# Spectral filter plus GELU network on one core: tiles 4 to 15 transposed by DMA, and the loads, first activations and order of work rearranged

## The chip, the cores and the metric

The kernel runs on one core of a Trainium2 chip. The metric is the device time in microseconds (us) of one execution; the median over the runs shown stands for a kernel. A profile is a hardware trace of one such execution. Its span runs from the first to the last recorded instruction, and the execution's own time is a little longer than the span.

## The reference

The input `x` is 2048 rows of 640 values in bfloat16. Each row is normalised (`xn`), and three terms are added:

```python
def _layernorm(x, axis=-1, eps=1e-5):
    m = jnp.mean(x, axis=axis, keepdims=True)
    v = jnp.var(x, axis=axis, keepdims=True)
    return (x - m) / jnp.sqrt(v + eps)

def _A_ref(x, w_r, w_i):                       # spectral filter over the whole 2048 x 640 plane
    X = rfft2(x.astype(float32), axes=(-2, -1))
    X = X * (w_r + 1j * w_i)                   # w: 2048 x 321
    return irfft2(X, s=(2048, 640), axes=(-2, -1)).astype(bfloat16)

def _B_ref(x, w1, b1, w2, b2):                 # w1: 640 x 1536, w2: 1536 x 640
    h = gelu(einsum("bsd,df->bsf", x, w1) + b1)
    return einsum("bsf,fd->bsd", h, w2) + b2

xn = _layernorm(x)
return x + _A_ref(xn, w_r, w_i) + _B_ref(xn, w1, b1, w2, b2)
```

## The kernel before

**Tiles.** The 2048 rows are held as 16 tiles of 128 rows (tile `c` holds the rows `16 p + c`, one for each partition `p`). All matrix work is in bfloat16 with float32 sums in PSUM, which has eight banks.

**Normalisation.** For each tile VectorE makes two `bn_stats` (line 622) and one `bn_aggr` (line 624), GpSimd takes the power -1/2 (line 626), and VectorE writes the normalised tile into a buffer `xn` that holds a pair of tiles (line 650; there are two such buffers). Tile 0 comes in two halves with a DMA each (lines 553 to 555), so that its first `bn_stats` can start on the first half. Tile 1's sums are made by ScalarE instead: two activations with accumulation (lines 583 and 585) and a small GpSimd instruction (line 587).

**The transposed copy.** Layer 1 needs each tile with its 640 columns on the partitions, as `xnT`, five blocks of 128 by 128. For tiles 0 to 7 TensorE makes five transposes into PSUM (line 667), and VectorE or ScalarE copies the result to `xnT` (line 673). Tiles in `BYDMA`, 8 to 15, are transposed by one DMA each, issued by SyncE (line 655), from `xn` straight to `xnT`.

**Layer 1 and the activation.** Layer 1 goes in blocks of tiles (`BLOCKS`): four blocks of two tiles (0 and 1, 2 and 3, 4 and 5, 6 and 7) and two blocks of four. For each of 12 chunks of the 1536 columns, five matmuls of 128 x 128 weights against 256 (or 512) columns of `xnT` are summed in one PSUM bank; ScalarE applies GELU with the bias into `gT` (line 738). In block 0 the first three of the five partial sums are made for each tile by itself (lines 710 to 716), the last two for both (line 727).

**The transform.** The two-dimensional transform is a chain of small matrix products with constant tables. VectorE folds each pair of normalised tiles (lines 679 and 683). TensorE multiplies the folded pair by the table G (line 689, the "table sums", `a_ops`), and the result is copied to `XV`. When all 16 tiles are there, the steps b (table E, line 762), c (table M, line 780), the filter on VectorE (lines 805 and 809), and d (table N, line 814) follow; 16 DMA transposes on SyncE (line 830) bring the result back into `XV`. The last part multiplies by the table GE (line 847), unfolds on VectorE (lines 855 and 860) and multiplies by H (line 913).

**Layer 2 and the output.** Layer 2 sums 12 products for each tile (`W2`, line 895). The residual and b2 come through buffers `xo`: ScalarE writes b2 into them as float32 (line 883), and a GpSimd DMA adds `x` (line 901). For tiles in `KEEP` the layer-2 sum is made early and VectorE adds it into `xo` (line 907), so that only the product with H is left for the end; for the others, layer 2 and H are summed in the same PSUM bank. VectorE adds `xo` and writes the output tile (line 916), and SyncE stores it (line 919).

**Loads.** All loads are written once, in order. SyncE issues `x`, `W1` and the tables in one queue; the eight direct loads of the filter (16 rows of 10,272 bytes each, `load_direct`) are issued by GpSimd once the load of tile 4 has landed (line 574). `W2` comes in four quarters, all behind tile 1's second activation, which uses `W2`'s space (line 600). Ten mirrored filter loads, GE and H follow among the DMA transposes (`turned`, line 604).

**What sets the order.** The order on each engine is written out by a list scheduler when the kernel is built (`Sched.schedule`): it takes a cost for each operation and a landing time for each DMA (`LAND`, line 173), and picks among the ready operations by priority (`PRIO`, `FOLD`, `GP`). `gate` only orders an operation behind the planned start of another; `reads`, `writes` and `after` become semaphore waits. On the chip each engine works through its own list strictly in order.

Of the kernel before, what the change touches and what calls it, by code (L numbers as in the profile page):

```python
# [13 lines left out]
D = 640  # L14
# [75 lines left out]
def mm_us(n):  # L90
    return max(n / 2400.0 + 0.0027, 0.0265)
# [81 lines left out]
LAND = {"x0_0#0": 2.21, "x0_1#0": 2.21, "x1#0": 2.41, "w1_0#0": 3.22, "b1t#0": 2.89, "w1_1#0": 3.98, "x2#0": 4.36, "w1_2#0": 4.71, "w1_3#0": 5.24, "w1_4#0": 5.77, "g#0": 6.59, "x4#0": 6.92, "x6#0": 7.12, "x8#0": 7.31, "x10#0": 7.5, "x12#0": 7.69, "x14#0": 8.04, "b2#0": 8.65, "e#0": 9.53, "m#0": 10.11, "n#0": 10.62, "W0#0": 5.52, "W0#1": 6.15, "W0#2": 6.54, "W0#3": 6.83, "W1#0": 6.67, "W1#1": 7.22, "W1#2": 7.12, "W1#3": 7.67, "w2#0": 13.91, "w2#1": 15.43, "w2#2": 16.32, "w2#3": 17.2, "W0#4": 2.91, "W0#5": 2.91, "W0#6": 3.32, "W0#7": 2.75, "W0#8": 2.84, "W1#4": 3.26, "W1#5": 3.67, "W1#6": 4.09, "W1#7": 3.51, "W1#8": 3.86, "i#0": 3.77, "h#0": 4.59, "xnT8#0": 2.89, "xnT9#0": 2.89, "xnT10#0": 3.31, "xnT11#0": 3.05, "xnT12#0": 3.15, "xnT13#0": 2.89, "xnT14#0": 2.89, "xnT15#0": 2.89, "v0#0": 2.89, "v1#0": 2.89, "v2#0": 2.89, "v3#0": 2.89, "v4#0": 2.89, "v5#0": 2.89, "v6#0": 2.89, "v7#0": 2.89, "v8#0": 2.89, "v9#0": 2.89, "v10#0": 2.89, "v11#0": 2.89, "v12#0": 2.89, "v13#0": 2.89, "v14#0": 2.89, "v15#0": 2.89, "xo0#0": 4.54, "out#0": 2.3, "xo1#0": 7.6, "out#1": 2.3, "xo2#0": 4.88, "out#2": 2.3, "xo3#0": 5.22, "out#3": 2.3, "xo4#0": 5.56, "out#4": 2.3, "xo5#0": 7.94, "out#5": 2.3, "xo6#0": 8.28, "out#6": 2.3, "xo7#0": 5.9, "out#7": 2.3, "xo8#0": 6.24, "out#8": 2.3, "xo9#0": 6.58, "out#9": 2.3, "xo10#0": 4.54, "out#10": 2.3, "xo11#0": 4.88, "out#11": 2.3, "xo12#0": 4.54, "out#12": 2.3, "xo13#0": 6.92, "out#13": 2.3, "xo14#0": 7.26, "out#14": 2.3, "xo15#0": 4.88, "out#15": 2.14, "out#16": 2.3, "out#17": 2.3}  # L173
# [231 lines left out]
BYDMA = tuple(range(8, 16))  # L405
# [6 lines left out]
XASPLIT = ['01234', '01 23 4', '0123 4', '01 234', '01 234', '01 234', '01 234', '01234']  # L412
KEEP = (0, 2, 3, 4, 7, 8, 9, 13, 14)
HOME = tuple(sorted((KEEP + tuple(c for c in range(16) if c not in KEEP))[-8:], key=lambda c: (c not in KEEP, c)))
FOLD = (14.0, 2.2, -51.6, -6.5, -36.5, 14.2, 44.0, 25.3)
GP = (-104.5, 12.2, 81.5, -77.1, 20.9, 158.1)
WARM = 42


def bass_parallel_sum__spectral_gfnet__dense_activation_gelu__prompt_kernel(  # L420
# [21 lines left out]
    with ExitStack() as es:  # L442
# [25 lines left out]
        mom = sb("mom", [128, 2], F32)  # L468
# [94 lines left out]
        load_w1(4)  # L563
        load(gtab[:], const["G"], B_g, (8, 4096), issue=0.5)
        load_x(4, 2)
# [16 lines left out]
        B_s1, B_s2, B_v1 = Buf("s1"), Buf("s2"), Buf("v1")  # L582
        K.op([("act", 0.75)], 300, lambda e, _: e.activation(view(W2, 0, [[1, D]]), view(X, D, [[1, D]]), ACT.Copy, scale=-1.0 / D, accum_out=mom[:, 0:1]),
             reads=[B_x[1]], writes=[B_s1])
        square = K.op([("act", 0.75)], 300, lambda e, _: e.activation(view(W2, 0, [[1, D]]), view(X, D, [[1, D]]), ACT.Square, bias=mom[:, 0:1], accum_out=mom[:, 1:2]),
                      reads=[B_x[1], B_s1], writes=[B_s2])
        K.op([("pool", 0.12)], 500, lambda e, _: e.tensor_scalar(out=mv[:, 1, 1:2], in0=mom[:, 1:2], scalar1=1.0 / D, scalar2=1e-5, op0=ALU.mult, op1=ALU.add),
             reads=[B_s2], writes=[B_v1])
# [3 lines left out]
        load(b2bc[:], bass.AP(tensor=b2v.tensor, offset=b2v.offset, ap=[[0, 128], [1, D]]), B_b2b, (8, 1280))  # L592
        load(etab[:], const["E"], B_e, (8, 1600))
        load(mtab[:], const["M"], B_m, (8, 512))
        load(ntab[:], const["N"], B_n, (8, 384))
        for ri in range(2):
            for q in range(4):
                load_direct(ri, q)
        for h in range(4):
            load_w2(h, after=[square])  # L600
        turned = [[] for _ in range(4)]
# [14 lines left out]
        for c0, n in [(0, 1), (1, 1)] + [(c, 2) for c in range(2, 16, 2)]:  # L616
            pr = 100 - c0 / 2
            B_mv, B_r = Buf("mv") if c0 != 1 else B_v1, Buf("r")
            for c in range(c0, c0 + n) if c0 != 1 else ():
                B_st = Buf("st")  # L620
                for h in range(2):
                    K.op([("dve", 0.393)], pr, lambda e, _, c=c, h=h: e.bn_stats(stats[:, c, 6 * h:6 * h + 6], view(X, c * D + H2 * h, [[1, H2]])),  # L622
                         reads=[B_x[c]] if c else [B_x0[h]], writes=[B_st], gate=mv_ops[:1])
                mv_ops.append(K.op([("dve", 0.119)], pr, lambda e, _, c=c: e.bn_aggr(mv[:, c, :], stats[:, c, :]), reads=[B_st, B_eps], writes=[B_mv]))  # L624
            a, b = c0, c0 + n
            K.op([("pool", 0.65)], 500, lambda e, _, a=a, b=b: e.tensor_tensor(out=rstd[:, a:b], in0=mv[:, a:b, 1], in1=mhalf[:, a:b], op=ALU.pow),  # L626
                 reads=[B_mv, B_mh], writes=[B_r] + B_rs[a:b])

        for pair in range(8):
# [10 lines left out]
            for n in range(2):  # L640
# [4 lines left out]
                for j0, j1 in cuts:  # L645
                    b = Buf(f"xn_{c}_{j0}")
                    for j in range(j0, j1):
                        B_xn[j] = b
                    w = 128 * (j1 - j0)
                    o = K.op([("dve", 0.356 if w == D else 0.1 + w / 1900)], pr, lambda e, _, c=c, n=n, xnv=xnv, o0=128 * j0, w=w: e.tensor_scalar(  # L650
                        out=xnv(n, o0, [[1, w]]), in0=view(X, c * D + o0, [[1, w]]), scalar1=mv[:, c, 0:1] if c != 1 else mom[:, 0:1], scalar2=rstd[:, c:c + 1], op0=ALU.subtract if c != 1 else ALU.add, op1=ALU.mult),
                        reads=([B_x[c]] if c else B_x0) + [B_rs[c]], writes=[xn, b])
                norm_ops.append(o)
                if c in BYDMA:
# [3 lines left out]
                    if c % 2 and c > 8:  # L658
                        turned[(c - 9) // 2].append(TD[c])
# [50 lines left out]
        for j in range(3):  # L710
            for c in range(2):
                first[j, c] = pe([("128", NFC * mm_us(128))], 60 - c - j / 4, lambda j=j, c=c: [
                    (h0v(fc, c, 1), view(W1, F * j + 128 * fc, [[1, 128]]), xnT[:, c, j, :], j == c == 0 and fc % 2 == 0, False) for fc in range(NFC)],
                    reads=[B_w1s[j], B_xnj[c, j]], writes=h0, gate=([first[j - 1, c]] if j else []) + ([first[j, 0]] if c else []))
                l1_ops.append(first[j, c])
                l1_of.setdefault(0, []).append(l1_ops[-1])
        for bi, (c0, nt) in enumerate(BLOCKS):
            for fc in range(NFC):
# [6 lines left out]
                if not bi:  # L725
                    if fc % 2 == 0:
                        l1_ops.append(pe([("128", 4 * mm_us(256))], pr + 10, lambda fc=fc: [
                            (h0v(f, 0, 2), view(W1, F * j + 128 * f, [[1, 128]]), xnT[:, 0:2, j, :], False, j == 4) for f in (fc, fc + 1) for j in (3, 4)],
                            reads=[B_w1s[3], B_w1s[4]] + [B_xnj[c, j] for c in range(2) for j in (3, 4)], writes=[hps], gate=[first[2, 1]]))
                        l1_of[0].append(l1_ops[-1])  # L730
                else:
# [6 lines left out]
                K.op([("act", act_us(128 * nt, 1))], pr + PRIO["gelu"] + GP[bi], lambda e, _, c0=c0, nt=nt, fc=fc, hps=hps: e.activation(  # L738
                    gT[:, fc, 128 * c0:128 * (c0 + nt)], psb(hps.slot, [[1, 128 * nt]]) if c0 else h0v(fc, 0, 2), ACT.Gelu_apprx_tanh, bias=b1col[:, fc:fc + 1], scale=1.0),
                    reads=[hps, B_b1c], writes=[bg])  # L740

# [217 lines left out]
```

## Time and profile before

| | |
|---|---|
| median of 3 runs | 150.87 us (150.87 to 151.32) |
| profiled execution: time | 150.26 us |
| profiled execution: span | 148.5 us |
| TensorE busy (matmul) | 141.8 us, 95% of the span |
| VectorE, ScalarE, GpSimd busy | 111.7, 82.7, 26.8 us |
| granted TensorE clock | 1.00 throughout |

In the profile PE is the TensorE matmul, PEld its weight load, DVE is VectorE, ACT ScalarE, POOL GpSimd and SP SyncE; a "q" behind a name is that engine's queue of issues. A group of instructions is shown as line, engine, operation, output<-inputs, count, then busy time and the mean in ns of one. Most matmuls are issued through one helper, so they share line 501 and are told apart by the tiles they read: `xnT,W` is layer 1, `W,gT` layer 2, `gtab,T` the table sums, `ident,T` the transposes. Matmul durations overlap one another, so the time that one takes in a run of matmuls is its share of that run and not its own duration.

### The profile page before, as it was taken

The page shows a single profiled execution, that of the slowest core. Times are in us where ns is not written, and L with a number is a line of the kernel's source. Part 1 is how long each engine was busy: PE and PEld are TensorE (multiplying, and loading weights), DVE is VectorE, ACT ScalarE, POOL GpSimd, SP SyncE. Part 2 cuts the span into 40 slices and gives each one's busy share as a digit, 9 for nine tenths or more (in the row PEclk, how much of TensorE's full clock was granted, in tenths as well). Part 3 has the DMA queues.
Part 4 walks back from the last instruction along what each step waited for, and adds up shares of the span by engine and source line. Part 5 has one row for each costly group of instructions (what it writes and reads, how often), then busy time and mean ns, then how long its engine had stood idle before and what let it go on. Part 6 is the DMA issues. An engine that isn't in the chain of part 4 may idle for free.

```text
span 148.5 us, 4149 instructions
## 1 busy us (share of the span) xinstructions
PE 141.8 (95%) x1740; PEld 92.5 (62%) x1756; DVE 111.7 (75%) x234; ACT 82.7 (56%) x151; POOL 26.8 (18%) x46
## 2 busy tenths in 40 slices
PE   7799999999999999999999999999999999999992
PEld 7589999988565536446553454444566765665572
DVE  2479999999994259857965995974019999999731
ACT  3526999999999994852658737444612240111000
POOL 4313830121200199700040000000040000000000
DMA  4999999999868979999934166063536113322221
GB/s 101 311 404 404 337 229 227 279 195 137 145 132 158 247 158 257 266 268 206 110 83 98 29 123 31 18 120 76 104 67 156 49 44 115 111 88 81 95 93 46
DMA packets 28307, 23.00 MB, mean 155 GB/s; under 512 B 17792, under 2 KB 24320, under 8 KB 28160
## 3 DMA queue, kind: packets, MB, share of 16 engines
q1 hardware_dynamic: 25696, 16.17, 46.6%
q0 software_dynamic: 2592, 6.56, 19.4%
q8 instruction: 14, 0.23, 0.7%
q14 instruction: 5, 0.04, 0.1%
HBM read 13.54 MB, written 2.62 MB: 109 GB/s over the span
## 4 chain that ended last, share of the span: by engine, by line
PE 88%; DVE 4%; DMA 3%; issue 2%; SPq 1%; ACT 0%
PE ps L501 87%; DMA W<-in_B_w_dram 3%; PE ps L667 1%; DVE Wf L513 1%; DVE Wf L855 1%; SPq L496 1%; DVE W L916 1%; DVE X L907 1%; DVE Wf L860 0%; ACT xnT L512 0%
## 5 line engine op out<-in xcount | busy, mean ns | idle before, releaser
L501 PE MATMUL ps<-xnT,W 128*128 128x256 bf16 (+2 forms) x396 | 57.0, 295 | 0.9 <-DMA W<-in_B_w_dram 0.9
L501 PE MATMUL ps<-W,gT 128*128 128x512 bf16 (+3 forms) x382 | 55.3, 292 | 1.5 <-issue 1.1
L501 PEld LDWEIGHTS ps<-W,gT 128*128 128x128 bf16 x396 | 30.1, 98 | 23.3 <-issue 2.2
L501 PEld LDWEIGHTS ps<-xnT,W 128*128 128x128 bf16 x396 | 34.1, 98 | 16.0 <-issue 1.7
L738 ACT ACTIVATE gT<-ps,b1col 128x256 bf16<-128x256 f32 (+1 forms) x72 | 37.4, 593 | 6.4 <-PE ps L501 6.1
L512 ACT ACTIVATE Wf<-ps 128x960 bf16<-128x960 f32 (+1 forms) x7 | 6.2, 894 | 22.0 <-PE ps L501 22.0
L901 POOL DMA_DIRECT2D xnT<-in_A_x_dram x8 | 9.9, 2596 | 45.4 <-DMA XV<-U 32.6
L622 DVE BATCH_NORM_STATS2 stats<-X 128x6 f32<-128x320 bf16 x30 | 13.1, 472 | 2.5 <-DMA X<-in_A_x_dram 2.5
L512 ACT ACTIVATE Xb<-ps 128x960 bf16<-128x960 f32 (+1 forms) x8 | 9.2, 1189 | 8.3 <-PE ps L501 8.3
L805 DVE TENSOR_TENSOR T<-Y,Wf 128x1288 bf16<-128x1288 bf16 x16 | 12.5, 826 | 0.0
L513 DVE CAST Y<-ps 128x644 bf16<-128x644 f32 x8 | 6.6, 828 | 6.2 <-PE ps L501 6.2
L513 DVE CAST Wf<-ps 128x960 bf16<-128x960 f32 (+1 forms) x5 | 5.1, 1019 | 7.5 <-PE ps L501 7.5
L626 POOL TENSOR_TENSOR rstd<-mv,mhalf 128x2 f32<-128x2 f32 (+1 forms) x9 | 6.6, 732 | 22.3 <-DVE mv L624 22.2
L916 DVE TENSOR_TENSOR W<-ps,xnT 128x640 bf16<-128x640 f32 (+2 forms) x10 | 6.9, 689 | 4.1 <-PE ps L501 4.1
L901 POOL DMA_DIRECT2D X<-in_A_x_dram x8 | 7.2, 2106 | 11.9 <-ACT gT L738 11.9
L683 DVE TENSOR_TENSOR T<-T 128x512 bf16<-128x512 bf16 (+1 forms) x32 | 8.5, 318 | 0.1
L512 ACT ACTIVATE XV<-ps 128x512 bf16<-128x512 f32 (+3 forms) x9 | 7.7, 873 | 0.0
L501 PE MATMUL ps<-getab,XV 32*128 32x160 bf16 (+1 forms) x128 | 7.5, 242 | 0.0
L512 ACT ACTIVATE U<-ps 128x512 bf16<-128x512 f32 (+1 forms) x12 | 4.6, 434 | 4.9 <-PE ps L501 4.8
L512 ACT ACTIVATE Y<-ps 128x644 bf16<-128x644 f32 x8 | 5.7, 707 | 2.9 <-PE ps L501 2.9
L513 DVE CAST Xb<-ps 128x640 bf16<-128x640 f32 (+1 forms) x4 | 4.3, 1065 | 3.9 <-PE ps L501 3.9
L907 DVE TENSOR_TENSOR X<-ps,X 128x640 f32<-128x640 f32 x8 | 6.6, 822 | 0.8 <-PE ps L501 0.8
(58 smaller groups left out, 149.6 us busy)
## 6 DMA issues: line engine op xcount, KB each, us to landing
X<-in_A_x_dram POOLq DMA_DIRECT2D x8, 320.0 KB, 6.7
xnT<-in_A_x_dram POOLq DMA_DIRECT2D x8, 320.0 KB, 7.8
out_dram<-W SPq DMA_DIRECT2D x15, 160.0 KB, 1.8
X<-in_A_x_dram SPq DMA_DIRECT2D x7, 320.0 KB, 8.8
W<-in_B_w_dram SPq DMA_DIRECT2D x5, 384.0 KB, 5.7
W<-in_B_w_dram SPq DMA_DIRECT2D x4, 480.0 KB, 18.4
Wf<-in_A_w_r_dram POOLq DMA_DIRECT2D x4, 160.5 KB, 8.4
Wf<-in_A_w_i_dram POOLq DMA_DIRECT2D x4, 160.5 KB, 9.6
```

Of the source, the lines that this page charges most:

```text
L496: return K.op([(q, 0.7 if q == "pool" else issue)], prio, lambda e, _: e.dma_start(dst, src), writes=[buf], after=after, rows=rows, gate=g ...
L501: ins = e.matmul(o_, lhsT=lw, rhs=rh, start=st, stop=sp_, skip_group_check=True)
L512: return e.activation(dst(), src(), ACT.Copy, scale=scale)
L513: return e.tensor_copy(dst(), src())
L622: K.op([("dve", 0.393)], pr, lambda e, _, c=c, h=h: e.bn_stats(stats[:, c, 6 * h:6 * h + 6], view(X, c * D + H2 * h, [[1, H2]])), reads=[B ...
L626: K.op([("pool", 0.65)], 500, lambda e, _, a=a, b=b: e.tensor_tensor(out=rstd[:, a:b], in0=mv[:, a:b, 1], in1=mhalf[:, a:b], op=ALU.pow), ...
L683: ring_ops.append(K.op([("dve", dve_us(4 * w, 2))], pr, lambda e, _, op=op, x1v=x1v, xfv=xfv, o_=o_, o0=o0, o1=o1, w=w: e.tensor_tensor(ou ...
L738: K.op([("act", act_us(128 * nt, 1))], pr + PRIO["gelu"] + GP[bi], lambda e, _, c0=c0, nt=nt, fc=fc, hps=hps: e.activation(gT[:, fc, 128 * ...
L805: filt_ops.append(K.op([("dve", dve_us(4 * KP, 2))], pr, lambda e, _, k=k, Y=Y, TB=TB, pair=pair: e.tensor_tensor(out=view(TT, TB.slot * 8 ...
L901: xo_ops[c] = K.op([("pool", 0.9)], 51 - c / 20, lambda e, _, c=c, xov=xov: e.dma_start(xov(0, D), xv[:, c, :], accum_op=ALU.add), reads=[ ...
L907: kept_ops.append(K.op([("dve", dve_us(D))], 30, lambda e, _, kps=kps, xov=xov: e.tensor_tensor(out=xov(0, D), in0=psb(kps.slot, [[1, D]]) ...
L916: K.op([("dve", dve_us(w))], 95, lambda e, _, os_=os_, fps=fps, o0=o0, w=w, xov=xov, base=base: e.tensor_tensor(out=view(W1, OST + os_.slo ...
```

## The change

- `BYDMA` is tiles 4 to 15 instead of 8 to 15: twenty TensorE transposes and four copies go, four DMA transposes on SyncE come.
- Tile 0 is loaded by one DMA. Tile 1's sums are made by VectorE like those of all other tiles; the two activations and the small GpSimd instruction go. All normalising writes are ordered behind tile 1's `bn_aggr`.
- The load of tiles 4 and 5 is issued ahead of the table G.
- The eight direct filter loads move from GpSimd to SyncE, and they, b2, E, M, N and the first quarter of `W2` are ordered behind the transposes of tiles 5 and 7 (`soon[1]`); the other quarters are ordered behind those of tiles 9, 11 and 13, and the mirrored filter loads one pair of tiles later than before.
- In block 0 of layer 1 the first partial sum of tile 0 is cut in two, and the fourth partial sum of the first six chunks is made ahead of the rest. The first table sum on TensorE is ordered behind the start of the tenth activation (`GATE0`).
- `KEEP` has ten tiles instead of nine, and others than before. Four of the `xo` additions wait for all 16 back transposes instead of two (and two for the first four).
- The planner's landing times (from issue to landing) are other ones: the first fifth of the layer-1 weights, `w1_0`, goes from 3.22 to 4.45 us, a tile's DMA transpose (`xnT8`) from 2.89 to 3.03, the last quarter of `W2` from 17.2 to 3.58. Priorities, the order of the transform's steps (`CHAIN`) and the splitting of copies (`XASPLIT`) change too.

```diff
-BYDMA = tuple(range(8, 16))
+BYDMA = tuple(range(4, 16))
...
-PRIO = {"hps": 50.5, "gelu": 116.3, "pb": 85.6, "pc": 135.6, "filt": 315.5, "ipc": 126.3, "eps": 84.4, "fin": 46.0}
+PRIO = {"hps": -20.8, "gelu": 180.6, "pb": 117.8, "pc": 194.1, "filt": 253.3, "ipc": 67.0, "eps": 51.3, "fin": 20.7}
 AHEAD = 1
-CHAIN = 'b0 b1 c01 c00 b2 c10 d00 d01 c11 b3 b4 c20 d11 c21 d10 b5 d20 c31 c30 d21 d30 d31'.split()
...
-KEEP = (0, 2, 3, 4, 7, 8, 9, 13, 14)
+CHAIN = 'b0 b1 c01 c00 b2 c10 d01 d00 c11 b3 d11 d10 b4 c21 c20 b5 c30 d20 c31 d21 d30 d31'.split()
...
+KEEP = (1, 2, 3, 4, 5, 8, 9, 11, 12, 14)
...
+GATE0 = 9
...
-        B_x0 = [Buf(f"x0_{h}") for h in range(2)]
-        for h in range(2):
-            load(view(X, H2 * h, [[1, H2]]), xv[:, 0, H2 * h:H2 * h + H2], B_x0[h], (8, 640), issue=0.41)
+        load_x(0, 1)
         load_x(1, 1)
...
+        load_x(4, 2)
         load(gtab[:], const["G"], B_g, (8, 4096), issue=0.5)
-        load_x(4, 2)
...
-                           bass.AP(tensor=src.tensor, offset=src.offset + q * RUN, ap=[[128 * 321, 16], [1, RUN]]), B_w[ri], (1, 10272), q="pool", after=[x_ops[4]], prio=90))
+                           bass.AP(tensor=src.tensor, offset=src.offset + q * RUN, ap=[[128 * 321, 16], [1, RUN]]), B_w[ri], (1, 10272), gate=soon[1]))
...
-            load_w2(h, after=[square])
+            load_w2(h, gate=[soon[1], turned[0], turned[1], turned[2]][h])
...
-            load_mirror(*a, gate=turned[(0, 0, 1, 1, 1, 2, 2, 2, 3, 3)[k]])
+            load_mirror(*a, gate=turned[(1, 1, 2, 2, 2, 3, 3, 3, 3, 3)[k]])
...
-                    if c % 2 and c > 8:
-                        turned[(c - 9) // 2].append(TD[c])
+                    if c % 2:
+                        (turned[(c - 9) // 2] if c > 8 else soon[1]).append(TD[c])
...
+        for j, c, f0, f1 in ((0, 0, 0, 6), (0, 0, 6, 12), (0, 1, 0, 12), (1, 0, 0, 12), (1, 1, 0, 12), (2, 0, 0, 12), (2, 1, 0, 12)):
...
+                reads=[B_w1s[j], B_xnj[c, j]], writes=h0[f0 // 2:f1 // 2], gate=prev)
...
+                if not bi and fc == GATE0:
+                    a_ops[0].gate.append(g_op)
...
-            xo_ops[c].deps += v_ops[:4] if c in HOME[4:6] else v_ops if c in HOME[6:] else []
+            xo_ops[c].deps += v_ops if c in HOME[4:] else []
```

More of the change, by code (lines that the diff above doesn't have):

```diff
@@ L467, in bass_parallel_sum__spectral_gfnet__dense_activation_gelu__prompt_kernel @@
         mhalf = sb("mhalf", [128, 16], F32)
-        mom = sb("mom", [128, 2], F32)
         rstd = sb("rstd", [128, 16], F32)
@@ L580, in load_mirror @@
                            bass.AP(tensor=src.tensor, offset=src.offset + row * 321, ap=[[128 * 321, 16], [-321, n], [1, 321]]), B_w[ri], (n, 642), issue=0.64, **kw))
[L582 to L588, printed above, removed]
         def load_w2(h, **kw):
             load(W2[:, 3 * h:3 * h + 3, :], w2v[:, 3 * h:3 * h + 3, :], B_w2, (24, 1280), **kw)
[L592 to L595, printed above, removed]
+        soon, turned = [[], []], [[] for _ in range(4)]
         for ri in range(2):
@@ L617, in bass_parallel_sum__spectral_gfnet__dense_activation_gelu__prompt_kernel @@
             pr = 100 - c0 / 2
-            B_mv, B_r = Buf("mv") if c0 != 1 else B_v1, Buf("r")
-            for c in range(c0, c0 + n) if c0 != 1 else ():
+            B_mv, B_r = Buf("mv"), Buf("r")
+            for c in range(c0, c0 + n):
                 B_st = Buf("st")
```

48 lines of the change are left out of this document (28 added, 20 removed).

## The prediction

> **What bounds the kernel now.** I read the page first: engine totals, slices, chain.
>
> ```profile
> span 148.5 us, 4149 instructions
> PE 141.8 (95%) x1740; PEld 92.5 (62%) x1756; DVE 111.7 (75%) x234; ACT 82.7 (56%) x151; POOL 26.8 (18%) x46
> PE   7799999999999999999999999999999999999992
> PE 88%; DVE 4%; DMA 3%; issue 2%; SPq 1%; ACT 0%
> ```
>
> PE has work in every slice and is 88% of the chain, so I looked for its idle time: the chain in order of time (start and length in us), then PE's waits from 8.9 to 146 us (total, times, longest).
>
> ```profile
> 2.13 4.29 DMA W<-in_B_w_dram
> 6.55 0.83 PE ps L501 x12
> 8.26 0.13 PE ps L667 x2
> ...
> 8.41 0.39 ACT xnT L512
> ...
> 8.85 3.40 PE ps L501 x53
> 12.25 0.56 PE ps L667 x10
> ...
> 17.55 0.28 PE ps L667 x5
> ...
> 18.05 0.28 PE ps L667 x5
> ...
> 20.85 0.28 PE ps L667 x5
> ...
> 23.54 0.28 PE ps L667 x5
> ```
>
> ```profile
> PE ps L501 <- issue: 1.1, 7, 0.2
> PE ps L501 <- ACT xnT L512: 0.3, 1, 0.3
> PE ps L501 <- DVE Wf L855: 0.2, 1, 0.2
> ```
>
> Layer 1 starts at 6.55, when W1's first part has landed; PE waits once more for tile 1's copy (8.39 to 8.85), and from then to the end it waits for others 0.2 us in all. So two things move the time: matmul work taken from PE, or a wait given to it. The windows view tells who runs close beside PE (busy us of PE, PEld, DVE, ACT, POOL; clock; DMA share; GB/s):
>
> ```profile
> 8.20:46.50 38.30, 37.99 (x399) 31.59 (x396) 36.91 (x113) 34.54 (x75) 9.50 (x15) 1.00 1.00 240
> 110.60:139.30 28.70, 28.13 (x273) 18.07 (x279) 28.50 (x44) 6.15 (x7) 0.54 (x1) 1.00 0.30 93
> 139.30:148.50 9.20, 6.40 (x60) 4.58 (x59) 2.79 (x5) 0.00 (x0) 0.00 (x0) 1.00 0.23 74
> ```
>
> VectorE is full from 8 to 46 us (36.91 of 38.30), where it prepares the tiles, and from 111 to 139 us, where it unfolds. After 139 PE alone sets the end, for some 6 us, which is the room that VectorE has there.
>
> **The parts.** The sum is made on the profiled execution, 150.26 us (span 148.5); the median of the runs is 0.61 above it, so the difference is taken from 150.87.
>
> *Transposes on PE.* Twenty go, for tiles 4 to 7: the four groups at 17.55, 18.05, 20.85 and 23.54, 4 x 0.28 = **-1.12**, all on the chain. Their four copies leave VectorE and ScalarE, beside PE's work.
>
> *Start.* One issue of SyncE less: W1's first part is issued 0.47 sooner, at 1.66, and lands at about 5.95.
>
> ```profile
> X<-in_A_x_dram SPq DMA_DIRECT2D x1, 80.0 KB, 2.0
> X<-in_A_x_dram SPq DMA_DIRECT2D x1, 160.0 KB, 2.6
> 2.71 0.98 DVE L622 BATCH_NORM_STATS2 stats<-X 128x6 f32<-128x320 bf16 x2 [1.79 <-DMA X<-in_A_x_dram]
> 3.73 0.22 DVE L624 BATCH_NORM_AGGREGATE mv<-stats 128x2 f32<-128x15 f32 x1
> 4.66 0.63 DVE L650 TENSOR_SCALAR T<-X,mv,rstd 128x256 bf16<-128x256 bf16 x2 [0.71 <-POOL rstd L626]
> 5.38 0.29 DVE L513 COPY xnT<-ps 128x256 bf16<-128x256 bf16 x1
> ```
>
> Tile 0 in one piece is 160 KB; between 2.0 (half of it) and 2.6 (tile 1, among more traffic) I take 2.3, so it lands at 3.0, and its sums end at 4.2. Tile 1's, now VectorE's (0.98 + 0.22), end at 5.3, with tile 1 landed at 1.20 + 2.6 = 3.8. Tile 0's normalising comes behind them: from its start to the end of the first copy was 5.67 - 4.66 = 1.0, so layer 1 can start at 6.2 to 6.3 instead of 6.55: **-0.35**, bounded by the whole issue (-0.47) and by a tile 1 that lands 0.5 late (+0.2). ScalarE loses two activations it spent on tile 1, which costs nothing there.
>
> *Tile 1's wait.* Its factor is ready 0.6 after 5.3, its normalising takes 0.45 on VectorE, transposes and copies 0.8 more: 7.2. PE, starting at 6.2 with 12 small matmuls in 0.83 and the five transposes between, asks at about 7.2. The 8.39 to 8.85 wait goes, **-0.46**, bounded by 0.
>
> *New waits of PE.* The moved tiles must still arrive in time. The rows: DMA issues with their size and us to landing (the first, fourth and last of tiles 8 to 15, then H's load), SyncE's, VectorE's and PE's instructions in time (start, length), and two groups (count, busy us, mean ns).
>
> ```profile
> xnT<-T SPq DMA_TRANSPOSE x1, 5.6
> xnT<-T SPq DMA_TRANSPOSE x1, 2.7
> xnT<-T SPq DMA_TRANSPOSE x1, 2.6
> htab<-c_H SPq DMA_DIRECT2D x1, 512.0 KB, 4.6
> 29.57 2.62 SPq L655 DMA_TRANSPOSE xnT<-T  x2
> 33.01 3.45 SPq L655 DMA_TRANSPOSE xnT<-T  x2
> 38.45 5.25 SPq L655 DMA_TRANSPOSE xnT<-T  x4
> 16.78 0.81 DVE L650 TENSOR_SCALAR T<-X,mv,rstd 128x640 bf16<-128x640 bf16 x2
> 32.13 0.80 DVE L650 TENSOR_SCALAR T<-X,mv,rstd 128x640 bf16<-128x640 bf16 x2
> L513 DVE COPY xnT<-ps 128x640 bf16<-128x640 bf16 x4 | 1.8, 482 | 0.0
> L501 PE MATMUL ps<-xnT,W 128*128 128x256 bf16 x52 | 5.8, 273 | 0.0
> 47.84 0.96 PE L501 MATMUL ps<-etab,XV 128*128 128x160 bf16 x16
> 55.71 1.58 PE L501 MATMUL ps<-W,gT 128*128 128x128 bf16 x11 [0.16 <-issue]
> ```
>
> When PE asks: the last matmuls of 256 columns, 52 after 33.0 us, took 5.8, so 0.107 each without the overlap of the last, and block 4 (tiles 8 to 11) began at 38.5. Block 0 is 72 matmuls of 128 columns and 15 transposes (ten take 0.56: 4.9) and 24 of 256 (2.6), so with a start at 6.25 block 1 begins near 14.0. Its 60 matmuls (6.4) and one set of ten table sums (0.56) later PE asks for tiles 4 and 5, at 20.9; at 28 for 6 and 7; for 8 to 11 at 38.5 - 1.9 = 36.6, with the three terms gained.
>
> When they come: the first of the eight DMA transposes landed 5.6 us after its issue, behind loads of W2; the last, with little ahead of it, 2.6; each holds SyncE 1.3. [...] In the new order W2, tables and filter stand behind tile 7, but the loads of x up to tile 15 still stand ahead. VectorE had tiles 4 and 5 normalised at 17.2 and 17.6; with G's load no longer ahead of x4 and with copies left out I take 1.1 sooner: tile 4 at 16.1, so tile 5's transpose starts at 17.5 and lands between 20.1 and 23.1, against 20.9. Tile 11 was normalised at 32.9. With two copies (0.4 each in a run) less and the pause before 8.2 filled, 1.3 sooner: its transpose starts at 32.8 and lands at 35.4, against 36.6. Both come close to the need. Before, the plan had W1 landing 3.22 us after its issue and the trace has 4.29, so PE ran 1.1 us behind its plan and the others had that much room; now the plan says 4.45, and the room is gone. Between 0 and +3.3 (the first rival) I take **+0.5**, nearer the 2.6 row, since the long row had W2 ahead of it.
>
> *SyncE's queue.* Eight filter loads, b2, E, M, N and W2's first quarter now wait behind tile 7's transpose, at some 24 us, and are issued at about 0.5 each, by 31. E is first used at 47.8, M, N and the filter follow it in the chain: 0, with over 10 us of cover. W2's last quarter comes behind tile 13's transpose, the second of the four from 38.45 on, and lands near 46 by the 4.6 of H's load, which is of like size; layer 2 began at 55.7, and block 4 alone is 60 matmuls of 512 columns, 12.8 us from 36.6 on. 0, but up to +1.0 if the new order starts layer 2 where the plan has W2 land (3.58 for 4.6). GpSimd loses eight issues and gains nothing that PE waits for.
>
> *Order at the end.* One more `KEEP` tile is one more addition on VectorE (L907, as long as the other additions, 0.8), ahead of the unfolding, and 3.2 us of layer 2 (12 x 640 columns) that PE can do while the back transposes run. 0, within -0.5 (some changes of tile shape less) and +1.0 (one place where PE waits). `GATE0` moves 0.56 us of PE work to where layer 1 gives way: 0. The two `xo` additions that now wait for the last back transposes join two that did already, and no wait of PE or of its VectorE neighbours in the rows above was on those: 0.
>
> Sum: -1.12 - 0.35 - 0.46 + 0.5 = -1.43; 150.26 becomes 148.8, and the median 150.87 becomes **149.4**.
>
> **Rivals.**
> *Tiles 4 and 5 come late* (slower). If VectorE is no sooner than before (17.2) and the transposes take 5.6 in the queue, tile 5 lands at 18.6 + 5.6 = 24.2, PE stands for 3.3 us from 20.9 on, and the time is 150.87 - 1.93 + 3.3 = 152.2. It decides from a landing at 22.8 on, where the wait eats the 1.93. For it speaks a full DMA (share 1.00 up to 46 us), against it that W2 no longer stands ahead. [...]
> *VectorE hides it* (no change). Tile 1's sums (1.2 us) find no pause on VectorE, and two copies (0.8) are all that it saves: tile 11 lands 0.4 later than the 37.9 of before (transpose issued at 35.2, 2.7 to landing), and PE, there at 36.6, stands for 1.7: 150.87 - 1.93 + 1.7 = 150.6. It decides from a VectorE that is no sooner than before; for it speaks that VectorE pauses for only 1.4 of these 38.3 us, against it that tile 1's sums fall ahead of them.
> *The new order waits elsewhere* (slower). The steps b to d, W2 or the last back transposes come later than PE has other work; each us is lost once, and a loss of 1.9 cancels the gain. Three such places of 1 us give 152.0. For it: the whole list is new. Against it: between 46 and 110 us the old list had no such wait.
>
> **How the numbers follow.** The forecast, waits of up to 1.3 us, 0.53: 148.3 to 150.3. Hidden, 0.09. Tiles late, 0.21; new order waits, 0.17, both slower. Runs of this kernel spread over 0.3%, 0.45 us, which I take as no change. Faster 0.53, same 0.09, slower 0.38. The range reaches from 150.87 - 1.12 - 0.47 - 0.46 - 0.5 = 148.3 to the late tiles' 152.2, rounded to 152.4 for the 0.2 at the start; the forecast's own range is 148.3 to 150.3.
>
> **What would show it.** The transposes from `ident` are 20 instead of 40. Layer 1's first matmul stands at 6.2 and none waits for tile 1 at 8. The DMA transposes of tiles 4 and 5 land by 21, tile 11's by 36.6; in PE's waits of 8.9 to 146 a DMA row on `xnT` of more than 1.9 us would make the prediction wrong, as would rows on W2 or `XV` of that size.

## The result: slower by 1.3%, and the profile after

The changed kernel takes 152.93 us (median of 4 runs, 152.76 to 153.42) against 150.87: the ratio is 1.0135, with a 95% interval of 1.0104 to 1.0166. The forecast of 149.4 was wrong, in sign too, and the time is above the 152.4 at which its range ends. The profiled execution has a span of 150.3 us against 148.5, so 1.8 us have to be found. All ratios compare undisturbed executions only, so a ratio need not be the quotient of the medians.

First the page of the changed kernel: span, engine totals, TensorE's slices, the chain.

```profile
span 150.3 us, 4104 instructions
PE 141.6 (94%) x1720; PEld 90.2 (60%) x1736; DVE 113.1 (75%) x238; ACT 79.0 (53%) x142; POOL 22.3 (15%) x37
PE   7799999989899999999998999999999999999993
PE 71%; DMA 12%; DVE 10%; issue 2%; SPq 2%; ACT 1%; POOL 1%; ACTq 0%
```

TensorE has 20 matmuls less, and it is still the bound, but its share of the chain fell from 88% to 71%, and DMA rose from 3% to 12%: a wait was given to it in several places. TensorE's waits over the whole span (total, times, longest; left out are the wait on `warm`, ahead of the work, and ten short pauses of 0.2 us or less for which the profile shows no releaser):

```profile
PE ps L657 <- DVE T L640: 0.8, 2, 0.6
PE ps L501 <- DMA xnT<-T: 0.7, 1, 0.7
PE ps L501 <- ACT U L512: 0.7, 1, 0.7
PE ps L501 <- ACT gT L735: 0.4, 1, 0.4
PE ps L501 <- DVE xnT L513: 0.3, 1, 0.3
```

And where they stand, from TensorE's timeline (start, length, group, and in brackets the idle time before it):

```profile
6.11 0.51 PE L501 MATMUL ps<-xnT,W 128*128 128x128 bf16 x6
...
7.37 4.80 PE L501 MATMUL ps<-xnT,W 128*128 128x128 bf16 x72 [0.34 <-DVE xnT L513]
12.37 0.81 PE L657 MATMUL ps<-ident,T 128*128 128x128 bf16 x10 [0.20 <-DVE T L640]
...
33.31 5.74 PE L501 MATMUL ps<-xnT,W 128*128 128x256 bf16 x45 [0.40 <-ACT gT L735]
39.77 1.89 PE L501 MATMUL ps<-xnT,W 128*128 128x512 bf16 x8 [0.73 <-DMA xnT<-T]
...
79.80 0.52 PE L501 MATMUL ps<-Z,ntab 32*32 32x320 bf16 x32 [0.69 <-ACT U L512]
```

Up to block 3 of layer 1 the change had gained: it began at 30.55 instead of 31.31. Block 4 (the 39.77 row) began 1.3 later than before (38.46). The brackets count from a modelled end of the last matmul and miss short pauses. So for the account I took from the trace each gap between two matmuls' starts, less the pace of an unbroken run (0.107 us for 256 columns):

| place | before | after | difference |
|---|---|---|---|
| layer 1's first matmul | 6.55 | 6.11 | -0.44 |
| transposes on TensorE, 40 and 20 | | | -1.12 |
| gaps up to 31 us (tiles 1 to 3, `W1`) | 0.67 | 1.34 | +0.67 |
| 32.6 to 35.5: ScalarE's `gT` late | 0 | 1.12 | +1.12 |
| 38.8: tile 11's transpose | 0.14 | 0.89 | +0.75 |
| 48.6: first of layer 2, cause open | 0 | 0.1 | +0.1 |
| 78.7: `U`, behind the first back transposes | 0 | 0.85 | +0.85 |
| sum | | | +1.9 |

What three of the last four rows wait for comes through SyncE's queue. (The gap at 48.6 is not W2's: its last quarter had landed at 48.33.) Its issues in time (start, length, count):

```profile
17.45 5.29 SPq L645 DMA_TRANSPOSE xnT<-T  x4
22.78 3.03 SPq L496 DMA_DIRECT2D Wf<-in_A_w_r_dram  x4
25.86 2.50 SPq L496 DMA_DIRECT2D Wf<-in_A_w_i_dram  x4
28.40 0.58 SPq L496 DMA_DIRECT2D b2bc<-in_B_b_dram  x1
...
30.45 2.62 SPq L645 DMA_TRANSPOSE xnT<-T  x2
33.12 0.58 SPq L496 DMA_DIRECT2D W<-in_B_w_dram  x1
33.74 3.06 SPq L645 DMA_TRANSPOSE xnT<-T  x2
...
44.14 0.58 SPq L496 DMA_DIRECT2D W<-in_B_w_dram  x1
```

From 17.45 to 51.7 SyncE issues without a pause. The eight filter loads hold it from 22.78 to 28.36, with b2, E, M and N to 30.41; only then comes the transpose of tile 8, although VectorE wrote that tile by 28.2 (its two instructions are the 27.80 row below). The rows of the chain in time show tile 8's and 9's normalising, tile 11's transpose and the second back transpose:

```profile
27.80 0.74 DVE T L640 x2
...
35.53 4.14 DMA xnT<-T
...
71.70 7.21 DMA XV<-U
```

Tile 11's transpose was issued at 35.53 (35.19 before) and took 4.1 instead of 2.7. b2, which before was issued at 8.97 and landed at 21.97, now landed at 32.13, and ScalarE, which writes b2 into the `xo` buffers in the midst of its GELU work, stood for it. VectorE stood for a `xn` buffer that a late transpose still had to read, and the last row is ScalarE's wait for the back transposes (timelines of the two engines):

```profile
32.15 0.74 ACT L882 ACTIVATE X<-b2bc 128x640 f32<-128x640 bf16 x1 [1.47 <-DMA b2bc<-in_B_b_dram]
...
37.15 0.80 DVE L640 TENSOR_SCALAR T<-X,mv,rstd 128x640 bf16<-128x640 bf16 x2 [1.67 <-DMA xnT<-T]
...
78.98 0.77 ACT L512 ACTIVATE U<-ps 128x512 bf16<-128x512 f32 x2 [3.08 <-DMA XV<-U]
```

The first back transposes took 7.2 to 7.5 us, 3.5 before. The twelve `xo` additions on GpSimd's queue, which in both kernels are issued ahead of them, began at 56.84 instead of 51.31: they wait for the mirrored filter loads, which SyncE now issues late (the last landed at 56.54, before at 51.01). That this made the transposes slow is what the variants with held additions test. DMA issues and GpSimd's timeline before, then GpSimd's timeline of the changed kernel:

```profile
XV<-U SPq DMA_TRANSPOSE x2, 3.5
```

```profile
51.31 7.24 POOL L901 DMA_DIRECT2D X<-in_A_x_dram  x8 [11.91 <-ACT gT L738]
```

```profile
56.84 7.18 POOL L900 DMA_DIRECT2D X<-in_A_x_dram  x8 [17.07 <-DMA Wf<-in_A_w_i_dram]
61.30 6.33 POOL L900 DMA_DIRECT2D xnT<-in_A_x_dram  x4
```

### The profile page after: what moved, and what is told of

The parts are those of the page before. It is cut to its first block, busy times and chain, and to the rows that moved or that the text cites. A ratio compares the mean times of both kernels' runs of the same rounds, so it can differ in the third digit from the quotient of the medians.

```text
span 150.3 us, 4104 instructions
## 1 busy us (share of the span) xinstructions
PE 141.6 (94%) x1720; PEld 90.2 (60%) x1736; DVE 113.1 (75%) x238; ACT 79.0 (53%) x142; POOL 22.3 (15%) x37
## 4 chain that ended last, share of the span: by engine, by line
PE 71%; DMA 12%; DVE 10%; issue 2%; SPq 2%; ACT 1%; POOL 1%; ACTq 0%
PE ps L501 71%; DMA XV<-U 5%; DMA X<-in_A_x_dram 4%; DVE stats L612 4%; DMA xnT<-T 3%; DVE T L640 1%; DVE T L673 1%; DVE XV L513 1%; SPq L496 1%; DVE T L669 1%; DVE mv L614 1%; PE ps L657 1%; ACT U L512 1%; POOL rstd L616 1%; ACT Y L512 0%
## 5 line engine op out<-in xcount | busy, mean ns | idle before, releaser
L501 PEld LDWEIGHTS ps<-xnT,W 128*128 128x128 bf16 x396 | 33.5, 98 | 19.8 <-ACT gT L735 4.8
L735 ACT ACTIVATE gT<-ps,b1col 128x256 bf16<-128x256 f32 (+1 forms) x72 | 35.6, 566 | 9.3 <-PE ps L501 9.0
L612 DVE BATCH_NORM_STATS2 stats<-X 128x6 f32<-128x320 bf16 x32 | 13.9, 470 | 2.9 <-DMA X<-in_A_x_dram 2.9
L512 ACT ACTIVATE Xb<-ps 128x960 bf16<-128x960 f32 (+1 forms) x9 | 9.8, 1138 | 8.2 <-PE ps L501 8.2
L512 ACT ACTIVATE Y<-ps 128x644 bf16<-128x644 f32 x9 | 6.3, 706 | 7.1 <-PE ps L501 7.1
L513 DVE CAST Y<-ps 128x644 bf16<-128x644 f32 x7 | 5.8, 829 | 5.3 <-PE ps L501 5.3
L640 DVE TENSOR_SCALAR T<-X,mv,rstd 128x640 bf16<-128x640 bf16 (+2 forms) x17 | 6.7, 430 | 2.1 <-DMA xnT<-T 1.7
L669 DVE TENSOR_TENSOR T<-T 128x640 bf16<-128x640 bf16 x16 | 7.3, 480 | 0.1
```

The source lines that it names most:

```text
L501: ins = e.matmul(o_, lhsT=lw, rhs=rh, start=st, stop=sp_, skip_group_check=True)
L512: return e.activation(dst(), src(), ACT.Copy, scale=scale)
L513: return e.tensor_copy(dst(), src())
L640: o = K.op([("dve", 0.356 if w == D else 0.13 + w / 1900)], pr, lambda e, _, c=c, n=n, xnv=xnv, o0=128 * j0, w=w: e.tensor_scalar(out=xnv( ...
L669: K.op([("dve", dve_us(640, 2))], pr, lambda e, _, k=k, op=op, xnv=xnv, x1v=x1v: e.tensor_tensor(out=x1v(H2 * k, [[D, 2], [1, H2]]), in0=x ...
L735: g_op = K.op([("act", act_us(128 * nt, 1))], pr + PRIO["gelu"] + GP[bi], lambda e, _, c0=c0, nt=nt, fc=fc, hps=hps: e.activation(gT[:, fc ...
```

## The experiments

*Theory:* the loss is the place of the loads in SyncE's one list; each thing that stands behind them there is late, and TensorE meets the late things one after the other. *Rival:* the new lists of the other engines (order, `KEEP`, twelve DMA transposes) cost by themselves. In all but one of the variants the edit is made on the finished plan, so every engine's list stays as it was except for what the diff moves. All variants compute the whole result. `xo_ops` holds the additions, `v_ops` the back transposes, `deps` what an operation waits for; `W0#` and `W1#` are loads of the filter's real and imaginary part, `w2#` the quarters of layer 2's weights. Two helpers are used: `at` finds a load by its name, `move` takes loads out of SyncE's list and puts them behind another.

```python
sp, pool = K.order["sp"], K.order["pool"]
def move(keys, behind):
    ops = [at(k) for k in keys]
    for o in ops:
        sp.remove(o)
    i = sp.index(at(behind)) + 1
    sp[i:i] = ops
```

**One wait taken away: b2 early.**

```diff
+move(["b2#0"], "x14#0")
```

> The changed kernel with its order on every engine kept, and only the load of b2 moved in SyncE's queue, from behind the eight filter loads to behind the last load of x. Theory (the waits stand in series): ScalarE's wait for b2 (1.5 us, until 32.1) and PE's 1.1 us of waits on ScalarE between 32 and 36 go, but PE then arrives 1.1 us sooner at tiles 8 to 11 and waits about 2.0 us there instead of 0.9: time within 0.3 us of the changed kernel's 152.9. Rival (the waits add up): 151.8.

Measured: 153.19 us, ratio 1.0126 (1.0075 to 1.0178), as slow as the change. ScalarE's wait and the three gaps at 32 to 36 are gone; TensorE came sooner to tile 11 and then to layer 2 and waited there (timeline of this variant):

```profile
38.14 1.89 PE L501 MATMUL ps<-xnT,W 128*128 128x512 bf16 x8 [0.90 <-DMA xnT<-T]
...
48.88 1.46 PE L501 MATMUL ps<-W,gT 128*128 128x512 bf16 x9 [1.72 <-ACT XV L512]
```

The second wait is put down to ScalarE, but W2's last quarter, issued at 44.15, landed at 48.79, and layer 2 began 0.09 later. So the waits stand in series: moving b2 alone gains nothing, since the next late load takes its place. The theory had put the new wait at tile 11 (2.0); there it was 0.9, and the rest came at W2 (1.7) and at the back transposes (1.3 at 80).

**Five loads out of the way of tile 8: E, M, N and W2's first quarter behind tile 11, b2 early.**

```diff
+move(["b2#0"], "x14#0")
+move(["e#0", "m#0", "n#0", "w2#0"], "xnT11#0")
```

> As the run with b2 early, and E, M, N and W2's first quarter moved behind the transpose of tile 11; the eight filter loads stay where they are. Theory (SyncE's queue holds tiles 8 to 11 up): tile 8's transpose starts at about 28.4 instead of 30.5, tile 11's lands by about 37 instead of 39.7, PE's waits between 32 and 39 go, 2.0 us: 150.9. Rival (VectorE or the DMA transposes themselves set tile 11's landing): it lands at 39 or later, 152.5 to 152.9.

Measured: 154.97 us, ratio 1.0267 (1.0223 to 1.0311), above both expected times; a miss. Up to block 4 it went as expected: tile 8's transpose was issued at 27.77, tile 11's landed at 35.44, and block 4 began at 36.9 without a wait. Then layer 2 stood for W2, which landed at 49.42 (timeline, then the windows: length, busy us of PE, PEld, DVE, ACT, POOL, granted clock, DMA share, GB/s):

```profile
49.52 0.69 PE L501 MATMUL ps<-W,gT 128*128 128x512 bf16 x2 [3.35 <-issue]
```

```profile
49.50:51.00 1.50, 1.49 (x6) 0.67 (x7) 0.00 (x0) 0.00 (x0) 0.00 (x0) 0.51 1.20 175
51.00:53.00 2.00, 2.00 (x11) 1.17 (x10) 0.00 (x0) 0.00 (x0) 0.00 (x0) 0.51 1.24 176
53.00:55.00 2.00, 2.00 (x25) 1.17 (x23) 0.89 (x1) 0.90 (x1) 0.00 (x0) 1.00 1.14 166
```

The wait of 3.4 us cost twice: for 3.5 us behind it the granted clock was 0.51, some 1.7 us more.

**The filter loads back on GpSimd's queue, behind the factor of tiles 6 and 7.**

```diff
+direct = [at(f"W{ri}#{q}") for ri in range(2) for q in range(4)]
+for o in direct:
+    sp.remove(o)
+    o.eng = "pool"
+i = max(k for k, o in enumerate(pool) if B_rs[7] in o.writes) + 1
+pool[i:i] = direct
```

> The changed kernel with its order kept, and only the eight direct filter loads moved from SyncE to GpSimd, behind the factor of tiles 6 and 7 (about 19.6 us). Theory (SyncE's queue): b2 lands by 27, tile 11 by 37, the mirrored filter loads and with them the xo additions about 4 us sooner, so that the back transposes no longer meet them: all three waits go, 1.1 + 0.9 + 0.85: 150.1. Rival (the DMA transposes are too slow whatever stands in the queue): 152.5 to 152.9.

Measured: 153.19 us, ratio 1.0151 (1.0082 to 1.0220); a miss. SyncE's queue was free of the filter loads, and yet the transposes came later. Those of tiles 4 to 7, issued at 16.7 to 20.7, landed after 2.7, 5.6, 9.4 and 12.3 us, the last three beside the filter loads on GpSimd's queue, and block 3 stood for tile 7 (DMA issues with us to landing, for tile 4 alone and for tiles 6 and 7 together; then the timeline):

```profile
xnT<-T SPq DMA_TRANSPOSE x1, 2.7
...
xnT<-T SPq DMA_TRANSPOSE x2, 10.9
```

```profile
33.09 0.49 PE L501 MATMUL ps<-xnT,W 128*128 128x256 bf16 x3 [2.06 <-issue]
```

b2 landed at 34.9 for the same reason. So it isn't only the place in the list: here DMA transposes were also late while another queue moved much at the same time (GpSimd's queue had 55.6% of the 16 engines from 17 to 26 us, and tile 7 took 12.3 us where tile 4, ahead of it, took 2.7).

**The filter loads early, in SyncE's idle time.**

```diff
+move(["b2#0"] + direct, "x14#0")
+move(["w2#0", "w2#1", "w2#2", "w2#3", "e#0"], "xnT7#0")
+move(["m#0", "n#0"], "xnT11#0")
```

> The changed kernel with its order kept on all engines but SyncE. There b2 and the eight filter loads are moved into the 8 us in which SyncE waits for tile 4 (behind the last load of x), the four quarters of W2 and E behind tile 7's transpose, M and N behind tile 11's. Theory (PE's waits at 32 to 36, 39, 46 to 49 and 79 are one chain that goes through SyncE's queue: b2, tiles 8 to 11, W2's last quarter, the mirrored filter loads and so the xo additions): all four go, tiles 4 and 5 land up to 0.5 us after PE asks at 22.9, tile 11 by 36, W2 by 35, the xo additions start by 52: about 149.8, faster than the kernel before. Rival (one cause each, and the transposes of tiles 4 and 5 now stand behind 1.3 MB of filter loads): tiles 4 and 5 land at 25 or later, and the time is 151.5 or more.

Measured: 155.29 us (median of four, 152.31 to 156.33) against 150.92. The one execution of 152.31 had the full clock, the other three a mean of 0.989. In the profiled execution (clock 0.989, 155.38 us) there is one wait only; behind it TensorE stands for nothing to the end (timeline):

```profile
27.29 3.63 PE L501 MATMUL ps<-xnT,W 128*128 128x256 bf16 x20 [4.35 <-DMA xnT<-T]
```

Tiles 4 and 5, issued at 16.7 and 18.0, landed at 25.1 and 27.2 behind 1.3 MB of filter. That is the first rival of the prediction, brought about by the edit: in this execution the late first tiles were paid in full, and behind the wait the granted clock was 0.75 (27.3 to 29.0 us), 0.50 (to 31.0) and 0.86 (to 33.0) on top. A variant that in addition leaves W2's last quarter behind tile 15 was meant to show whether W2 can come later still:

```diff
-move(["w2#0", "w2#1", "w2#2", "w2#3", "e#0"], "xnT7#0")
+move(["w2#0", "w2#1", "w2#2", "e#0"], "xnT7#0")
```

> As the run with the refilled queue, but W2's last quarter stays behind tile 15's transpose, as in the changed kernel. Theory (chain): everything up to 45 us as in that run; layer 2's first matmuls, which read all of W2, wait 1.5 to 2.5 us for that quarter, and the time is that much above that run: about 151.8. Rival (W2's place does not matter): the same time as that run.

Measured: 154.41 us, ratio 1.0193 (1.0094 to 1.0291), with the same wait on `xnT` (4.0) and none on W2. With TensorE that late, nothing can be said on W2.

**Fewer additions ahead of the back transposes.** Seven of the twelve early `xo` additions also wait for the first four back transposes.

```diff
+for c in (8, 9, 11, 12, 14, 0, 6):
+    xo_ops[c].deps = xo_ops[c].deps + v_ops[:4]
```

> The changed kernel with its order kept; of the twelve xo additions that GpSimd issues in a row, the last seven wait for the first four back transposes. Theory (the additions fill the DMA queues while the first back transposes run, so these take 7 us, ScalarE waits 3.1 us for a buffer and PE 0.85 at 78.7): the transposes land in about 3 us, the wait goes, 152.1. Rival (the wait has another cause, or VectorE now waits for the later additions): 152.9 or more.

Measured: 153.72 us, ratio 1.0156 (1.0101 to 1.0212); a miss in time. The profiled execution is the longest of the four (span 153.0, the others 150.6 to 151.7), so the sizes of its waits are upper ends. The first back transposes took 2.6 us instead of 7.2 and the wait at 78.7 is gone, but the additions now ran beside the next four (DMA issues from 80 to 95, then the timeline):

```profile
XV<-U SPq DMA_TRANSPOSE x2, 14.1
XV<-T SPq DMA_TRANSPOSE x2, 8.5
```

```profile
99.22 0.50 PE L501 MATMUL ps<-Xb,mtab 32*32 32x322 bf16 x32 [1.71 <-ACT U L512]
```

**The transposes of tiles 4 to 7 back on TensorE**, with a new plan for all engines.

```diff
-BYDMA = tuple(range(4, 16))
+BYDMA = tuple(range(8, 16))
```

> The changed kernel with only its first part undone: tiles 4 to 7 turned by TensorE again, and the order written anew by the planner. With no transposes of tiles 5 and 7 to stand behind, the filter loads, b2, the tables and W2's first quarter follow the loads of x at once. Theory (SyncE's queue between tiles 7 and 8 is what costs, not the planner's new numbers): tile 8's transpose is no longer held up, PE gets its 1.1 us of transposes back: 150.5 to 151.5. Rival (the new priorities and order cost by themselves): 153 or more.

Measured: 157.88 us, ratio 1.0432 (1.0341 to 1.0524); a miss. Its waits are other ones (1.8 before layer 2, where W2 landed at 47.4, 1.6 at 57 on an `xo` addition, 2 more from 118 on), because the planner laid out every engine anew. It doesn't isolate the transposes; it shows that with the priorities of the change another plan can be worse still.

**All of SyncE's list in a better order**, with nothing else touched: what is small goes into the idle time behind the last load of x, W2 and half of the filter between tiles 7 and 8, the rest behind tile 11.

```diff
+move(["b2#0", "e#0", "m#0", "n#0"], "x14#0")
+move(["w2#0", "w2#1", "W0#0", "W0#1", "W0#2", "W0#3", "w2#2"], "xnT7#0")
+move(["w2#3", "W1#0", "W1#1", "W1#2", "W1#3"], "xnT11#0")
```

> The changed kernel, every other engine's list as it is, and only SyncE's list put so that nothing stands late: b2, E, M and N in its idle time behind the last load of x, three quarters of W2 and four filter loads between the transposes of tiles 7 and 8, W2's last quarter and the other four filter loads behind tile 11. Theory (the place of the loads in SyncE's one list is the whole loss up to layer 2): tile 11's transpose lands by 36.9 (39.68 in the changed kernel), no wait of TensorE on ScalarE at 32 to 36, none of over 0.3 on xnT at the start of block 4, none on W2 at 46 to 49. The wait near 79 for the first back transposes stays, 0.9 to 1.5, since the mirror loads and the additions come no earlier. Sum: 150.3 + 0.6 (outside the span) and less 1.1, 0.6 and 0.3 of waits: 150.4 to 151.0. Rival (waits in series: TensorE only meets the next one; or the new lists of the other engines cost by themselves): 152.5 to 153.5.

Measured: ratio 0.9999 (0.9967 to 1.0030), span 148.7, as the theory expected. The times of the twelve executions spread widely (150.03 to 155.67, median 151.87), but the median of their spans, 148.9, is that of the kernel before in the same comparison, 148.9. In this profile block 4 began at 37.2 without a wait, W2 was there by 39.2, and all of 31 to 39 us is one run; what is left is the wait for the back transposes, since the mirrored loads are still late and the additions still began at 55.0 (timeline, then TensorE's waits from 8.9 to 146 us):

```profile
31.00 8.11 PE L501 MATMUL ps<-xnT,W 128*128 128x256 bf16 x65
39.39 0.73 PE L501 MATMUL ps<-gtab,T 128*128 128x128 bf16 x10 [0.28 <-DVE T L673]
```

```profile
PE ps L501 <- ACT U L512: 1.1, 1, 1.1
PE ps L501 <- DVE T L673: 0.3, 1, 0.3
```

The order of one engine's list, with the same loads and the same lists elsewhere, took the whole loss back. It moves the issues and the traffic together; which of the two weighs more, the runs don't separate. The sibling with W2's first quarter early in place of E, M and N:

```diff
-move(["b2#0", "e#0", "m#0", "n#0"], "x14#0")
+move(["b2#0", "w2#0"], "x14#0")
-move(["w2#0", "w2#1", "W0#0", "W0#1", "W0#2", "W0#3", "w2#2"], "xnT7#0")
+move(["w2#1", "W0#0", "W0#1", "W0#2", "W0#3", "w2#2"], "xnT7#0")
-move(["w2#3", "W1#0", "W1#1", "W1#2", "W1#3"], "xnT11#0")
+move(["w2#3", "W1#0", "W1#1", "W1#2", "W1#3", "e#0", "m#0", "n#0"], "xnT11#0")
```

> As the other reordered list, with W2's first quarter instead of E, M and N in the idle time behind the last load of x (0.49 MB instead of 0.32 ahead of the transposes of tiles 4 and 5), and E, M and N behind tile 11. Theory: if what stands ahead of tiles 4 and 5 is too much, they land after 23.4, where TensorE asks for them, and it waits there, 0 to 1.0; W2 is complete earlier; 150.5 to 151.5. Rival as there: 152.5 to 153.5.

Measured: ratio 1.0032 (0.9993 to 1.0071), span 148.7, median of the twelve spans 149.0; tile 5 landed at 20.8, so 0.49 MB of W2 ahead of it did no harm, where 1.3 MB of filter did (27.2).

**The suspected cause put into the kernel before**: its eight direct filter loads in SyncE's list behind tile 9's transpose, nothing else.

```diff
+for o in direct:
+    pool.remove(o)
+    o.eng = "sp"
+i = sp.index(at("xnT9#0")) + 1
+sp[i:i] = direct
```

> The kernel before, with one thing of the change alone: the eight direct filter loads are in SyncE's list, behind the transpose of tile 9, all other lists as they are. Theory (a transpose that stands behind eight loads is late by what they hold SyncE and the DMA engines): tile 10's transpose is issued some 5 us later (33.0 to 38), tile 11 lands at 42 to 43.5 (37.9 before), TensorE, which asks at 38.5, waits 3.5 to 5: 154 to 156. Rival (SyncE's list has cover, as the prediction said): 150.5 to 151.5.

Measured: 157.10 us, ratio 1.0436 (1.0374 to 1.0497). Tile 10's transpose was issued at 40.1 and tile 11's landed at 44.6; TensorE, which asked for them at 39.4, stood for it (timeline):

```profile
44.66 1.87 PE L501 MATMUL ps<-xnT,W 128*128 128x512 bf16 x4 [5.09 <-DMA xnT<-T]
```

The wait hit the upper end of what was expected; the time is above it by 1. The granted clock was 0.50 from 44.6 to 46.0 us and 0.61 to 48.0, which cost some 1.5 us, and in this execution TensorE also stood for 1.2 at 17 behind a load of `x` that landed 1.1 later than before, far ahead of the edit.

**The better order, and the last two or the last four early additions held** behind the first back transposes.

```diff
+for c in (0, 6):                 # the other variant: (12, 14, 0, 6)
+    xo_ops[c].deps = xo_ops[c].deps + v_ops[:4]
```

> The reordered list of SyncE (b2, E, M, N early, filter loads and W2 spread), and the additions of tiles 0 and 6, the last two of the twelve early ones, also wait for the first four back transposes, as two did in the kernel before. Theory (the first back transposes take 9.26 and 7.60 us because the twelve additions are still under way until 74.6): the additions end near 72, the first back transposes land near 73.5 to 74.5 instead of 76.6, TensorE's wait of 1.25 at 76.7 goes or keeps at most 0.4; the two held additions run at 75 to 78, ahead of the next back transposes: span 147.5 to 148.0, ratio 0.992 to 0.996. Rival (the next back transposes come late instead, as when seven were held): no gain, 0.998 to 1.005.

> The same with four additions held (tiles 12, 14, 0 and 6). Theory: the early additions end near 69, the first back transposes land near 71, no wait at 76.7; the four held ones run from about 72 to 78 and just clear the next back transposes, issued at 79.6: span 147.4 to 147.9, ratio 0.990 to 0.995. Rival: they reach past 79.6, and the next back transposes take 6 us or more, with a wait of TensorE near 92: 0.998 to 1.01.

Measured: ratio 0.9933 (0.9901 to 0.9965) with two held and 0.9944 (0.9920 to 0.9968) with four, spans 147.9 and 147.7. Both are faster than both kernels. Against the kernel before it is less than 1%, but the intervals leave 1 out. The views of TensorE's waits from 8.9 to 146 us, with two held:

```profile
PE ps L501 <- issue: 1.4, 9, 0.2
PE ps L501 <- DVE T L673: 0.7, 1, 0.7
```

The wait for `U` is gone in both. With four held, the next back transposes took 9.1 us for the first, as the rival said, but TensorE had other work and didn't wait.

## Why the prediction was wrong, point by point

- *Transposes on PE, -1.12:* right. 20 are left, and the account closes with this term to 0.1 us.
- *Start, -0.35:* right; 6.11 in the changed kernel's profile (-0.44, inside the bound of -0.47). In the variants' profiles it was 6.2 to 6.4.
- *Tile 1's wait, -0.46:* wrong, 0. The larger part of tile 1's copy now comes from VectorE, and TensorE stands for it at 6.85 for 0.52 (bracket 0.34 in the 7.37 row): it came there sooner by as much as the copy did. Two more short gaps (0.28, 0.37) follow, on `W1` and the normalising of tiles 2 and 3.
- *New waits, +0.5:* the first rows were right, the last was wrong. Tiles 4 and 5 landed at 20.1 and 21.5, inside the forecast's 20.1 to 23.1, and weren't waited for; the block that reads them began at 23.4. The forecast had it begin at 20.9, with one set of table sums ahead of it; the trace has two and a half between the starts of blocks 1 and 2, and in the kernel before the block began at 24.2. So the first rival's wait was priced too high (3.3, by 23.4 it would be 0.8). Tile 11 landed at 39.7, not 35.4. The transpose was priced as issued when VectorE is done (32.8; VectorE was done at 31.6), and SyncE's queue was not asked whether it is free: the issue came 2.7 late, and the landing took 4.1 instead of 2.6.
- *SyncE's queue, 0:* this is the step that failed. Twelve of the loads were through at 30.4, for "by 31", but by luck: they began 1.2 sooner than was taken (22.8 for 24) and a filter load held SyncE for 0.63, not 0.5. W2's first quarter came at 33.1. The main fault is another one: the cover of "over 10 us" was that of the engines that read these loads. What stands behind them in the same list was left out: b2 for ScalarE at 30.7, the transposes of tiles 8 to 11, W2 and, by way of the mirrored loads and the `xo` additions, the back transposes. That is 1.12 + 0.75 + 0.85 = 2.7 us, where the forecast had 0 here and 0.5 for new waits. With the 1.1 us by which tile 1's term and the short gaps behind it were off, 2.7 - 0.5 + 1.1 = 3.3 covers the distance of 3.2 us between the forecast's -1.43 and the +1.8 of the spans. The better order of that list alone gave 1.6 us of span back, with two held additions 2.4.
- *W2's last quarter, 0 to +1.0:* the forecast saw 46 against a layer 2 that began at 55.7. It landed at 48.33, and the new order has layer 2 at 48.96, so the cover of 10 us was gone and it was just in time. In the variant with seven additions held, with the same list on SyncE, layer 2 did wait for it (landed at 50.27, begun at 50.36); without the earlier waits it is the next wait (1.7 with b2 early, 3.4 with tile 8 early as well).
- *Order at the end, 0:* right behind 80 us: no new gap there. The one at 78.7 stands on additions that began 5.5 us later; twelve of them come early in both kernels. Changes of tile shape, which the bound of -0.5 counted on, did not become fewer: both traces have 58; the step from 128*128 to 32*32 takes 0.09 us above the pace in both (0.309 us from start to start instead of 0.216).
- *The rivals:* the third, three waits of 1 us in new places, is what happened; its mechanism was wrong in part, since the lists of the other engines, kept as they are, run with hardly a wait once SyncE's is put right. That VectorE hides the gain was not seen in the changed kernel: it was itself held for 1.67 us at 37.15 (the row above), by a buffer that a late transpose had not read yet. The first rival came only in the two variants that put the filter loads ahead of these tiles.

With both edits, the order of SyncE's list and two additions held, the change is worth 0.7% (ratio 0.9933), some two thirds of what was forecast. Tile 1's gap, and, with two held, 0.9 us at 38.7 where a table sum waits for VectorE's fold, remain. Whether a new order of VectorE's list would gain these was not tried.

## What to carry to other kernels

SyncE's queue worked through its list in order, like an engine (tile 8, written by 28.2, was issued at 30.45, behind twelve loads). When loads are moved in such a list, price what stands behind them in it, not only who reads them. The waits of the bound engine stood in series here, and taking one away showed only the next (1.0126 with b2 early, 1.0135 without); look for the common list behind them and mend that as a whole. What worked here was to put small loads into the queue's idle time and large ones where the transfers that must be quick are through (span 148.7 for 150.3), and what failed was 1.3 MB ahead of such a transfer (tile 5 at 27.2).

## What the runs showed of the hardware

**DMA transposes against another queue.** The share of the 16 engines that each queue had while the first back transposes were under way (q0 is GpSimd's, q1 SyncE's; 67 to 75 us), with their median time to landing, in the changed kernel and with four additions held:

```profile
q0 software_dynamic: 837, 1.89, 100.1%
q1 hardware_dynamic: 462, 0.12, 14.9%
XV<-U SPq DMA_TRANSPOSE x2, 7.3
```

```profile
q1 hardware_dynamic: 2683, 0.66, 69.0%
q0 software_dynamic: 94, 0.20, 10.4%
XV<-U SPq DMA_TRANSPOSE x2, 2.8
```

Between the two, with two held and q0 at 46.0%, they took 4.8. In the changed kernel's 8 us q1 moved 0.12 MB in 462 packets, q0 1.89 MB in 837. How the engines are shared out between the queues these rows don't show.

**The clock behind a long wait.** Behind TensorE's waits of 3.4, 4.4 and 5.1 us the granted clock was at or near 0.50 for some 3 to 3.5 us (0.51 for 3.5 us; 0.75, 0.50 and 0.86 in stretches of 1.7, 2 and 2 us; 0.50 for 1.4 and 0.61 for 2 us). With the wait of 4.0 (W2's last quarter behind tile 15) it was 8, 5 and 7 tenths in the three slices of 3.9 us from 23.2 us on, and 0.978 over the span. In the profiles of the variants whose longest wait was 1.7 or 2.1 us the mean clock of the span was 0.999 to 1.000. So in these profiles the clock was lower behind each wait of 3.4 us or more and behind none of up to 2.1; no wait in between was seen.

**An issue of a filter load** (16 rows of 10 KB) held SyncE 0.63 us from one start to the next in the changed kernel (the first 1.2), that of a table 0.47, a tile's transpose 1.3 (tiles 4 to 7).
